# A linear-attention and SwiGLU block: the first two x tiles as column halves ahead of the K weights, and the sum of phi(k) over tiles on GpSimd and VectorE

## The chip, the cores and the metric

The kernel runs on one core of a Trainium2 chip. The metric is the device time of one launch in microseconds (us). Three runs of the kernel before gave 224.91, 223.82 and 224.68 us, a median of 224.68 us. Besides these there is one profiled execution, from which all the views of the profile come.

A core has five engines that run side by side and meet at semaphores: TensorE (PE in the profile; its weight loads are listed apart as PEld), VectorE (DVE), ScalarE (ACT), GpSimd (POOL) and SyncE (SP), which here only issues DMAs. ScalarE issues a few DMAs too. An entry such as SPq or ACTq is the issuing of a DMA by that engine.

## The reference

The input x has 2048 tokens (S) of 512 features (D), in bf16. After a layernorm without scale, two blocks read the same normalised xn, and their outputs are added to x:

```python
def phi(t): return where(t > 0, t + 1, exp(t)) + 1e-6

xn = layernorm(x)                               # eps 1e-5
q, k, v = split(xn @ wqkv)                      # 32 heads of 16
pq, pk = phi(q), phi(k)
kv  = einsum("bhsd,bhse->bhde", pk, v)
z   = einsum("bhsd->bhd", pk)                   # the sum over all tokens
num = einsum("bhqd,bhde->bhqe", pq, kv)
den = einsum("bhqd,bhd->bhq", pq, z) + 1e-6
attn = (num / den) @ wo
ffn  = (silu(xn @ w_gate) * (xn @ w_up)) @ w_down   # F = 1792
out  = x + attn + ffn
```

The change touches z, the sum of phi(k) over the tokens, and the way in which the first x tiles reach the core.

## The kernel before, in words

Tokens lie in 16 tiles of 128 (NT = 16) on the partitions of the on-chip memory. The program is a list of operations. `K.add(engine, fns, r, w)` puts an operation at the end of one engine's instruction stream and derives the semaphore waits from the keys that it reads and writes. So the order in which the Python calls stand is the order on each engine; nothing is reordered later, and an instruction whose wait is not over holds up all that stands behind it on its engine.

**Loads.** The lines from 188 on issue the loads of x and of the weights of K and Q. Tile 0 comes as two column halves, one on SP's queue and one on ACT's. Then SP issues the K weights (`wload("sp", 1)`, 512 KB), tile 3, the Q weights (`wload("sp", 0)`, 512 KB), and tiles 6 to 15. ACT issues tiles 1, 2, 4 and 5, 128 KB each.

**First stage, tiles 0 to 3.** For each tile VectorE computes the statistics (`bn1`, `bn2`, lines 230 and 233), ScalarE the reciprocal standard deviation (`rs`, lines 237 and 239), VectorE the normalised tile (`lna_dve`, line 243). TensorE transposes it in four pieces (`transp`, line 261), and ScalarE evicts the result into xnT (`evac`, line 268). The K projection of the tile follows (`kproj`, line 299: four matmuls). VectorE's order in this stage is: statistics 0, statistics 1, normalisation 0, aggregation 1, statistics 2, normalisation 1, statistics 3, normalisation 2, normalisation 3. TensorE's is: transposes 0, transposes 1, K projection 0, transposes 2, K projection 1, transposes 3, K projections 2 and 3. Ahead of all this TensorE runs NWARM = 9 matmuls on zeros (line 222).

**Middle stage, steps s = 4 to 17.** From tile 4 on GpSimd normalises (`lna_pool`, lines 248 and 251), and a DMA transposes (`dmat`, line 276). A step s has the K projection of tile s, a Q projection (`qproj`, line 310), and the accumulation of xn^T times phi(k) of tile s - 2 in banks 0 to 3 (`gacc`, line 317). phi takes three engines: ScalarE the exponential (line 289), GpSimd the minimum with 1 (line 290), VectorE the combination with the projection in PSUM (line 293). Projections write banks 4 to 7 in turn, so a bank is written again two steps later. Tile 15 is the last that GpSimd normalises, at step 11; from step 12 on it has two minima a step.

**Last stage.** 56 pairs j of gate and up matmuls run (`gu(j)`, line 421: eight matmuls), 14 to each chunk of 512 tokens. ScalarE takes silu of the gate part (line 425), and VectorE multiplies with the up part (`hop(j)`, line 430). The rest of the attention is placed between the pairs:

- after pair 1, `z_sum` (line 454): 16 matmuls with a matrix of ones sum phi(k). Each of the four column groups of TensorE's array takes every fourth tile, and 32 output rows hold the same sum, so bank 1 holds four partial sums, 32 rows each. ScalarE copies it as bf16 (`zhi`), VectorE forms the remainder (`zlo`, line 459). Then `kv_mm` (line 444) with VectorE's mask (line 448);
- after pair 2, `z_mm` (line 466): eight 128x128 matmuls against a matrix of 1/32 (four groups, times zhi and zlo), whose results VectorE spreads into the block columns `Zc` (line 471); then `m_mm` (line 493), of which two follow pair 3;
- after pair 4, `den_mm` (line 476: 16 matmuls), ScalarE's copy (line 480), and four reciprocals on VectorE (`recip`, line 485), each followed by GpSimd's split into rhi and rlo (lines 486 and 487);
- after pairs 7, 10, 13 and 16, `bc_mm` (line 500): the reciprocals are broadcast, and `pqn` (line 508) multiplies them into phi(q), in this pair and the two behind it.

From the second chunk on, `otile` (lines 513 and 517) computes one output tile of the chunk before after the pairs 5, 8, 10 and 13 of a chunk (`O_SLOT`); VectorE adds x (line 523), and SP writes the tile out. The last four tiles follow at the end.

Of the kernel before, what the change touches and what calls it, by code (L numbers as in the profile page):

```python
# [20 lines left out]
HPG = P // DH  # L21
NH = D // DH

NWARM = 9
O_SLOT = {5: 0, 8: 1, 10: 2, 13: 3}


class _Program:
# [76 lines left out]
def bass_parallel_sum__linear_attn_block__swiglu_ffn__prompt_kernel(nc, A_x, A_wqkv, A_wo, B_x, B_w_gate, B_w_up, B_w_down, out):  # L105
    xin = A_x[0]
    oview = out[0]
    K = _Program()
    bf, f32 = dt.bfloat16, dt.float32

    with contextlib.ExitStack() as es:
        E = es.enter_context

        def sb(name, shape, dtype):
            return E(nc.sbuf_tensor(name, shape, dtype))
# [9 lines left out]
        pk = sb("pk", [P, NT, D], bf)  # L125
        pqT = sb("pqT", [P, NG, S], bf)
        hT = sb("hT", [P, 2, NFC, 512], bf)
        zhi = sb("zhi", [P, D], bf)
        zlo = sb("zlo", [P, D], bf)
        ef = sb("ef", [P, 4, D], bf)  # L130
        GT = sb("GT", [P, NDC, D], bf)
        kvT = sb("kvT", [P, NG, P], bf)
# [7 lines left out]
        sil = sb("sil", [P, 2, 512], bf)  # L140
        out_sb = sb("out_sb", [P, 2, D], bf)
        ident = sb("ident", [P, P], bf)
        ones = sb("ones", [P, 32], bf)
        ones32 = sb("ones32", [P, P], bf)
        maskt = sb("maskt", [P, P], bf)
        mask8 = sb("mask8", [P, HPG], bf)
        warm = sb("warm", [P, 512], bf)
# [37 lines left out]


        K.add("act", lambda e: e.preload_act_table_set("natural_log_exp_and_others"))
        for h, eng in ((0, "sp"), (1, "act")):
            load(eng, ("x", 0, h), x_sb[:, 0, h * 256:h * 256 + 256], xin[0:P, h * 256:h * 256 + 256])
        xload("act", 1)  # L190
        wload("sp", 1)
        xload("act", 2)
        xload("sp", 3)
        xload("act", 4)
        wload("sp", 0)
        xload("act", 5)
# [20 lines left out]
        blockmask(("mask8",), mask8[:, :], mask8[:, :], [])  # L217
        K.add("pool", lambda e: e.memset(eps6[:, :], 1e-6), w=[("eps6",)])
        K.add("pool", lambda e: e.memset(ones[:, :], 1.0), w=[("ones",)])
        K.add("pool", lambda e: e.memset(ones32[:, :], 1.0 / 32), w=[("ones32",)])  # L220
        K.add("pool", lambda e: e.memset(Zc[:, :, :], 0.0), w=[("Zc",)])
        K.add("pe", [(lambda e: e.matmul(banks[0][:, :], warm[:, 0:P], warm[:, :], start=True, stop=True))
                     for _ in range(NWARM)], r=[("warm",)], w=[B(0)])


        def xk(t):
            return [("x", t)] if t else [("x", 0, 0), ("x", 0, 1)]

        def bn1(t):
            K.add("dve", lambda e: e.bn_stats(stats[:, t, :], x_sb[:, t, :]), r=xk(t), w=[("st", t)])  # L230
# [91 lines left out]
        def eb_copy(q):  # L322
            sl = slice(32 * q, 32 * q + 32)
            dst = Eb[sl, :].rearrange("p (h e) -> p h e", e=DH)
            src = ident[sl, sl][:, :, None].broadcast_to([32, NH, DH])
            K.add("act", lambda e: e.activation(dst, src, ACT.Copy), r=[("ident",)], w=[("Eb", q)])

        def norm(t):
            bn1(t)
            bn2(t)  # L330
            rs(t)
            lna_pool(t)
            dmat(t)
# [54 lines left out]
        for s in range(4, NT + 2):  # L388
            prev, ends = ends, []
            if s < NT:  # L390
                ends.append(kproj(s))
            for e_ in prev:
                e_()
            for i in SQ[s]:
                ends.append(qproj(i))
            gacc(s - 2)
            if s + 4 < NT:
                norm(s + 4)
            if s in AL:
                AL[s]()  # L400
            if s > 12:
                for e_ in ends:
                    e_()
                ends = []
            if 12 <= s <= 15:
                eb_copy(s - 12)

        for h in (1,):
            fload("sp", "wg", wg, B_w_gate, h)
# [18 lines left out]
        def hop(j):  # L428
            C, fc = j // NFC, j % NFC
            K.add("dve", lambda e: e.tensor_tensor(  # L430
                out=hT[:, C % 2, fc, :], in0=banks[gb(j) + 1][:, :], in1=sil[:, j % 2, :], op=ALU.mult),
                r=[B(gb(j) + 1), ("sil", j % 2)], w=[("hT", C % 2, fc)])


        def gt_evac(c, eng):
            if eng == "act":
                K.add("act", lambda e: e.activation(GT[:, c, :], banks[c][:, :], ACT.Copy), r=[B(c)], w=[("GT", c)])
            else:
                K.add("dve", lambda e: e.tensor_copy(GT[:, c, :], banks[c][:, :]), r=[B(c)], w=[("GT", c)])
# [10 lines left out]
                in1=maskt[:, :][:, None, :].broadcast_to([P, NG, P]), op=ALU.mult),  # L450
                r=[B(0), ("maskt",)], w=[("kvT",)])

        def z_sum():
            K.add("pe", [(lambda e, q=q, t=t: e.matmul(
                banks[1][32 * q:32 * q + 32, :], ones[:, 0:32], pk[:, 4 * t + q, :],
                start=(t == 0), stop=(t == NT // 4 - 1))) for t in range(NT // 4) for q in range(4)],
                r=[("pk", t) for t in range(NT)] + [("ones",)], w=[B(1)])
            K.add("act", lambda e: e.activation(zhi[:, :], banks[1][:, :], ACT.Copy), r=[B(1)], w=[("zhi",)])
            K.add("dve", lambda e: e.tensor_tensor(out=zlo[:, :], in0=banks[1][:, :], in1=zhi[:, :], op=ALU.subtract),
                  r=[B(1), ("zhi",)], w=[("zlo",)])  # L460

        def z_mm():
            fns = []
            for g in range(NG):
                for i, z in enumerate((zhi, zlo)):
                    fns.append(lambda e, g=g, z=z, i=i: e.matmul(
                        banks[1][:, g * P:(g + 1) * P], z[:, g * P:(g + 1) * P], ones32[:, :],
                        start=(i == 0), stop=(i == 1)))
            K.add("pe", fns, r=[("zhi",), ("zlo",), ("ones32",)], w=[B(1)])
# [12 lines left out]

        def recip(q):
            sl = slice(q * P, (q + 1) * P)
            K.add("dve", lambda e: e.reciprocal(rd[:, sl], den[:, sl]), r=[("den",)], w=[("rd", q)])  # L485
            K.add("pool", lambda e: e.tensor_copy(rhi[:, sl], rd[:, sl]), r=[("rd", q)], w=[("rhi", q)])
            K.add("pool", lambda e: e.tensor_tensor(out=rlo[:, sl], in0=rd[:, sl], in1=rhi[:, sl], op=ALU.subtract),
                  r=[("rd", q), ("rhi", q)], w=[("rlo", q)])
# [40 lines left out]
        def otile(t):  # L529
            b = t % 4  # L530
            ogroup(b, t, 0, D)
            oout(b, t, 0, D)

        gt_evac(1, "act")
        gt_evac(0, "dve")
        gt_evac(2, "act")
        gt_evac(3, "dve")
        for j in range(NGU):
            C, fc = j // NFC, j % NFC
            gu(j)  # L540
            if j == 0:
                hop(j)
            elif j == 1:
                z_sum()
                kv_mm()
                hop(j)
            elif j == 2:
                z_mm()
                hop(j)
                m_mm(0)  # L550
                m_mm(1)
            elif j == 3:
                m_mm(2)
                m_mm(3)
                hop(j)
            elif j == 4:
                den_mm()
                hop(j)
                recip(0)
                recip(1)  # L560
            elif j == 5:
                hop(j)
                recip(2)
                recip(3)
            elif j in (7, 10, 13, 16):
                g = (j - 7) // 3
                bc_mm(g)
                hop(j)
                pqn(g, 0)
            else:  # L570
                hop(j)
                if j in (8, 11, 14, 17):
                    pqn((j - 8) // 3, 1)
                    pqn((j - 8) // 3, 2)
                if j in (9, 12, 15, 18):
                    pqn((j - 9) // 3, 3)
# [65 lines left out]
```

## Time and profile before

| what | us |
|---|---|
| median of three runs | 224.68 |
| lowest and highest run | 223.82, 224.91 |
| the profiled execution, its own time | 223.8 |
| its span in the trace | 222.1 |
| GpSimd busy | 35.6 |
| VectorE busy | 101.1 |
| ScalarE busy | 70.0 |

The span is shorter than the device time of the same execution by 1.7 us. The mean granted clock of TensorE over the span is 0.992. The page's row of DMA traffic shows 166 and 356 GB/s in the first two of 40 slices of 5.55 us, and 57 to 63 GB/s in the next three. The issues of the first loads read as follows (issue, time to landing): the halves of tile 0, 2.1 us on SP and 2.2 us on ACT; tile 1, 4.1 us; the K weights, 4.7 us; tile 3, 4.7 us; the Q weights, 6.8 us.

How to read what follows. A row of the timeline has the start, the length, the engine, the line of the kernel, the operation, the output and the inputs with their shapes, the count, and in brackets how long the engine idled before and what ended it. A row of the chain of waits has the start, the length and the engine with its line. A row of the windows gives for each engine the busy time and the number of instructions in that stretch, then TensorE's granted clock as a share of full speed, the busy share of the DMA engines and what they moved. Engines that idle off the chain cost nothing.

### The profile page before, as it was taken

To read this page: it belongs to the slowest core of one execution; us is meant where nothing else is said; L and a number is where in the kernel's file an instruction comes from. 1 tells how busy PE (TensorE), PEld (TensorE's weight loads), DVE (VectorE), ACT (ScalarE), POOL (GpSimd) and SP (SyncE) were. 2 spreads that over 40 slices of the span, in tenths; PEclk is the share of its full clock that TensorE was granted. 3 is DMA by queue.
4 is the path that set the end of the run, shared out by engine and by line. 5 is a ranking of instruction groups with operands and counts; after the bars stand their busy time and mean duration, and the time that the engine had idled before them with its cause. 6 is when DMAs were issued, how large, how long until landed. Compare 5 with 4: busy or idle time off the path is not lost.

```text
span 222.1 us, 2733 instructions
## 1 busy us (share of the span) xinstructions
PE 213.2 (96%) x1043; PEld 97.2 (44%) x1063; DVE 101.1 (46%) x170; ACT 70.0 (32%) x138; POOL 35.6 (16%) x81
## 2 busy tenths in 40 slices
PE   6699999999999999999999999999999999999995
PEld 2344334444543444444444444444444444444454
DVE  2876888555549777733223232422424232232121
ACT  3593566666463322213103131311313220130000
POOL 4069697643005000000000000000000000000000
PEclk9699999999999999999999999999999999999999
DMA  5922399997000000000000000000000000000101
GB/s 166 356 63 57 63 230 258 241 383 226 0 0 3 0 0 0 3 0 24 24 0 27 24 0 0 24 23 3 25 24 0 3 24 0 25 24 3 47 24 47
DMA packets 17485, 13.55 MB, mean 61 GB/s; under 512 B 7232, under 2 KB 17472, under 8 KB 17472
## 3 DMA queue, kind: packets, MB, share of 16 engines
q1 hardware_dynamic: 16752, 12.78, 20.0%
q10 hardware_dynamic: 720, 0.59, 0.8%
q8 instruction: 8, 0.13, 0.3%
q14 instruction: 5, 0.04, 0.1%
HBM read 9.70 MB, written 2.10 MB: 53 GB/s over the span
## 4 chain that ended last, share of the span: by engine, by line
PE 83%; POOL 5%; DMA 4%; DVE 3%; issue 2%; ACT 1%; POOLq 0%; ACTq 0%
PE pb L421 41%; PE pb L517 22%; PE pb L513 6%; PE pb L299 4%; PE pb L310 3%; PE pb L317 3%; DMA xnT<-xn 2%; DMA x_sb<-in_A_x_dram 2%; POOL xn L251 2%; POOL ef L290 2%; PE pb L500 1%; DVE rd L485 1%; DVE stats L230 1%; PE pb L261 1%; PE pb L476 0%
## 5 line engine op out<-in xcount | busy, mean ns | idle before, releaser
L425 ACT ACTIVATE sil<-pb 128x512 bf16<-128x512 f32 x56 | 33.3, 597 | 103.8 <-PE pb L421 102.6
L430 DVE TENSOR_TENSOR hT<-pb,sil 128x512 bf16<-128x512 f32 x56 | 38.6, 688 | 47.2 <-PE pb L421 46.4
L421 PE MATMUL pb<-xnT,wg 128*128 128x512 bf16 x221 | 57.0, 379 | 0.3 <-issue 0.2
L421 PE MATMUL pb<-xnT,wu 128*128 128x512 bf16 x216 | 55.9, 379 | 0.4
L517 PE MATMUL pb<-wd,hT 128*128 128x512 bf16 (+1 forms) x233 | 50.7, 366 | 0.3
L517 PEld LDWEIGHTS pb<-wd,hT 128*128 128x128 bf16 x238 | 23.3, 98 | 25.1
L523 DVE TENSOR_TENSOR out_sb<-pb,x_sb 128x512 bf16<-128x512 f32 (+1 forms) x17 | 11.2, 660 | 49.9 <-PE pb L517 49.9
L421 PEld LDWEIGHTS pb<-xnT,wu 128*128 128x128 bf16 x224 | 21.9, 98 | 26.4
L421 PEld LDWEIGHTS pb<-xnT,wg 128*128 128x128 bf16 x224 | 21.5, 98 | 27.1 <-issue 2.1
L290 POOL TENSOR_SCALAR ef<-ef 128x512 bf16<-128x512 bf16 x32 | 19.5, 615 | 17.0 <-ACT ef L289 16.8
L289 ACT ACTIVATE ef<-pb 128x512 bf16<-128x512 f32 x32 | 18.6, 591 | 8.6 <-PE pb L310 4.6
L299 PE MATMUL pb<-wqkv,xnT 128*128 128x512 bf16 x63 | 17.2, 400 | 0.8 <-DMA xnT<-xn 0.7
L513 PE MATMUL pb<-M,pqT 128*128 128x512 bf16 (+1 forms) x68 | 16.6, 366 | 0.0
L317 PE MATMUL pb<-pk,xn 128*128 128x512 bf16 x62 | 16.2, 379 | 0.3 <-DVE pk L293 0.2
L310 PE MATMUL pb<-xnT,wqkv 128*128 128x512 bf16 x63 | 16.2, 379 | 0.1
L293 DVE SCALAR_TENSOR_TENSOR pk<-pb,ef 128x512 bf16<-128x512 f32 x16 | 10.9, 689 | 7.9 <-POOL ef L290 7.6
L293 DVE SCALAR_TENSOR_TENSOR pqT<-pb,ef 128x512 bf16<-128x512 f32 x16 | 10.9, 689 | 5.2 <-POOL ef L290 5.1
L230 DVE BATCH_NORM_STATS2 stats<-x_sb 128x6 f32<-128x512 bf16 x16 | 10.9, 684 | 3.5 <-DMA x_sb<-in_A_x_dram 3.5
L508 DVE TENSOR_TENSOR pqT<-pb,pqT 128x512 bf16<-128x512 f32 x16 | 10.6, 681 | 0.2 <-PE pb L500 0.2
L299 PEld LDWEIGHTS pb<-wqkv,xnT 128*128 128x128 bf16 x64 | 6.3, 103 | 8.6 <-DVE mv L233 0.9
L513 PEld LDWEIGHTS pb<-M,pqT 128*128 128x128 bf16 x68 | 6.6, 98 | 7.4
L317 PEld LDWEIGHTS pb<-pk,xn 128*128 128x128 bf16 x64 | 6.2, 98 | 8.0 <-DVE pk L293 0.7
(60 smaller groups left out, 75.3 us busy)
## 6 DMA issues: line engine op xcount, KB each, us to landing
out_dram<-out_sb SPq DMA_DIRECT2D x15, 128.0 KB, 1.7
wg<-in_B_w_gate_dram SPq DMA_DIRECT2D x2, 896.0 KB, 6.0
wu<-in_B_w_up_dram SPq DMA_DIRECT2D x2, 896.0 KB, 7.2
wd<-in_B_w_down_dram SPq DMA_DIRECT2D x2, 896.0 KB, 11.4
wqkv<-in_A_wqkv_dram SPq DMA_DIRECT2D x3, 512.0 KB, 4.7
x_sb<-in_A_x_dram SPq DMA_DIRECT2D x11, 128.0 KB, 5.7
x_sb<-in_A_x_dram ACTq DMA_DIRECT2D x4, 128.0 KB, 5.4
wo<-in_A_wo_dram SPq DMA_DIRECT2D x1, 512.0 KB, 4.5
```

Of the source, the lines that this page charges most:

```text
L230: K.add("dve", lambda e: e.bn_stats(stats[:, t, :], x_sb[:, t, :]), r=xk(t), w=[("st", t)])
L289: K.add("act", lambda e: e.activation(buf, banks[b][:, :], ACT.Exp), r=[B(b)], w=[bkey])
L290: K.add("pool", lambda e: e.tensor_scalar(out=buf, in0=buf, scalar1=1.0 + 1e-6, scalar2=0.0, op0=ALU.min, op1=ALU.max), r=[bkey], w=[bkey])
L293: return lambda: K.add("dve", lambda e: e.scalar_tensor_tensor(out=dst, in0=banks[b][:, :], scalar=1e-6, in1=buf, op0=ALU.max, op1=ALU.add ...
L299: K.add("pe", [(lambda e, c=c: e.matmul(banks[b][:, :], xnT[:, c, t * P:(t + 1) * P], wqkv[:, c, D:2 * D], start=(c == 0), stop=(c == NDC ...
L310: K.add("pe", [(lambda e, c=c: e.matmul(banks[b][:, :], wqkv[:, c, g * P:(g + 1) * P], xnT[:, c, C * 512:(C + 1) * 512], start=(c == 0), s ...
L317: K.add("pe", [(lambda e, c=c: e.matmul(banks[c][:, :], xn[:, t, c * P:(c + 1) * P], pk[:, t, :], start=(t == 0), stop=(t == NT - 1))) for ...
L421: K.add("pe", [(lambda e, c=c, b=b, w_=w_: e.matmul(banks[b][:, :], w_[:, c, fc * P:(fc + 1) * P], xnT[:, c, C * 512:(C + 1) * 512], start ...
L425: K.add("act", lambda e: e.activation(sil[:, j % 2, :], banks[gb(j)][:, :], ACT.Silu), r=[B(gb(j))], w=[("sil", j % 2)])
L430: K.add("dve", lambda e: e.tensor_tensor(out=hT[:, C % 2, fc, :], in0=banks[gb(j) + 1][:, :], in1=sil[:, j % 2, :], op=ALU.mult), r=[B(gb( ...
L513: fns = [(lambda e, g=g: e.matmul(banks[bank][:, 0:hi - lo], pqT[:, g, t * P:(t + 1) * P], M[:, g, lo:hi], start=(g == 0), stop=False)) fo ...
L517: fns = [(lambda e, fc=fc: e.matmul(banks[bank][:, 0:hi - lo], hT[:, C % 2, fc, jj * P:(jj + 1) * P], wd[:, fc, lo:hi], start=False, stop= ...
```

## The change

Two parts are changed.

The loads: tiles 0 and 1 both come as two column halves, one half on each of the two queues, and all four stand ahead of the K weights. Tile 3 moves from SP's queue to ACT's, behind tile 2. NWARM goes from 9 to 10.

```diff
-NWARM = 9
-O_SLOT = {5: 0, 8: 1, 10: 2, 13: 3}
+NWARM = 10
+O_SLOT = {7: 0, 9: 1, 11: 2, 13: 3}
...
-        for h, eng in ((0, "sp"), (1, "act")):
-            load(eng, ("x", 0, h), x_sb[:, 0, h * 256:h * 256 + 256], xin[0:P, h * 256:h * 256 + 256])
-        xload("act", 1)
+        for t in (0, 1):
+            for h, eng in ((0, "sp"), (1, "act")):
+                load(eng, ("x", t, h), x_sb[:, t, h * 256:h * 256 + 256], xin[t * P:(t + 1) * P, h * 256:h * 256 + 256])
         wload("sp", 1)
         xload("act", 2)
-        xload("sp", 3)
+        xload("act", 3)
```

The sum of phi(k): GpSimd adds tiles 0 to 9 in fp32 (nine adds, one in each of the steps 12 to 17 and three behind the last step), VectorE tiles 10 to 15 (five adds, behind the hops of pairs 1 to 3) and then both halves into a bf16 tile `zb`, behind the hop of pair 4. What is left for TensorE is the sum over the 128 partitions: four 128x128 matmuls against ones, behind pair 5. zhi, zlo and the 16 matmuls of `z_sum` go.

```diff
+        NZP = 10
+        def z_add(half, i):
+            acc, key = zacc[:, half, :], ("zacc", half)
+            t = NZP * half + i
+            first, fkey = (pk[:, t - 1, :], ("pk", t - 1)) if i == 1 else (acc, key)
+            K.add("dve" if half else "pool",
+                  lambda e: e.tensor_tensor(out=acc, in0=first, in1=pk[:, t, :], op=ALU.add),
+                  r=[fkey, ("pk", t)], w=[key])
...
+            if s >= 12:
+                z_add(0, s - 11)
...
-        def z_sum():
-            K.add("pe", [(lambda e, q=q, t=t: e.matmul(
-                banks[1][32 * q:32 * q + 32, :], ones[:, 0:32], pk[:, 4 * t + q, :],
-                start=(t == 0), stop=(t == NT // 4 - 1))) for t in range(NT // 4) for q in range(4)],
...
+        def z_bf():
+            K.add("dve", lambda e: e.tensor_tensor(out=zb[:, :], in0=zacc[:, 0, :], in1=zacc[:, 1, :], op=ALU.add),
+                  r=[("zacc", 0), ("zacc", 1)], w=[("zb",)])
...
         def z_mm():
-            for g in range(NG):
-                for i, z in enumerate((zhi, zlo)):
-                    fns.append(lambda e, g=g, z=z, i=i: e.matmul(
-                        banks[1][:, g * P:(g + 1) * P], z[:, g * P:(g + 1) * P], ones32[:, :],
-                        start=(i == 0), stop=(i == 1)))
+            K.add("pe", [(lambda e, g=g: e.matmul(
+                banks[1][:, g * P:(g + 1) * P], zb[:, g * P:(g + 1) * P], ones[:, :], start=True, stop=True))
+                for g in range(NG)], r=[("zb",), ("ones",)], w=[B(1)])
...
+        for i in range(7, NZP):
+            z_add(0, i)
```

What stands behind each pair moves accordingly: `kv_mm` stays behind pair 1, `m_mm` behind pairs 2 and 3, `z_mm` goes from pair 2 to pair 5, `den_mm` from pair 4 to pair 6, the reciprocals from pairs 4 and 5 (two each) to pairs 6 (one), 7 (two) and 8 (one), the four `bc_mm` from pairs 7, 10, 13 and 16 to pairs 10, 13, 16 and 19, and the output tiles of a chunk from pairs 5, 8, 10 and 13 to pairs 7, 9, 11 and 13.

```diff
             elif j == 1:
-                z_sum()
                 kv_mm()
                 hop(j)
+                z_add(1, 1)
             elif j == 2:
-                z_mm()
-                hop(j)
                 m_mm(0)
                 m_mm(1)
+                hop(j)
+                z_add(1, 2)
+                z_add(1, 3)
...
             elif j == 4:
+                hop(j)
+                z_bf()
+            elif j == 5:
+                z_mm()
+                hop(j)
+            elif j == 6:
                 den_mm()
                 hop(j)
                 recip(0)
+            elif j == 7:
+                hop(j)
                 recip(1)
-            elif j == 5:
-                hop(j)
                 recip(2)
+            elif j == 8:
+                hop(j)
                 recip(3)
-            elif j in (7, 10, 13, 16):
-                g = (j - 7) // 3
+            elif j in (10, 13, 16, 19):
+                g = (j - 10) // 3
                 bc_mm(g)
```

More of the change, by code (lines that the diff above doesn't have):

```diff
@@ L127, in bass_parallel_sum__linear_attn_block__swiglu_ffn__prompt_kernel @@
         hT = sb("hT", [P, 2, NFC, 512], bf)
-        zhi = sb("zhi", [P, D], bf)
-        zlo = sb("zlo", [P, D], bf)
+        zacc = sb("zacc", [P, 2, D], f32)
+        zb = sb("zb", [P, D], bf)
         ef = sb("ef", [P, 4, D], bf)
@@ L142, in bass_parallel_sum__linear_attn_block__swiglu_ffn__prompt_kernel @@
         ident = sb("ident", [P, P], bf)
-        ones = sb("ones", [P, 32], bf)
-        ones32 = sb("ones32", [P, P], bf)
+        ones = sb("ones", [P, P], bf)
         maskt = sb("maskt", [P, P], bf)
@@ L219, in bass_parallel_sum__linear_attn_block__swiglu_ffn__prompt_kernel @@
         K.add("pool", lambda e: e.memset(ones[:, :], 1.0), w=[("ones",)])
-        K.add("pool", lambda e: e.memset(ones32[:, :], 1.0 / 32), w=[("ones32",)])
         K.add("pool", lambda e: e.memset(Zc[:, :, :], 0.0), w=[("Zc",)])
@@ L226, in xk @@
         def xk(t):
-            return [("x", t)] if t else [("x", 0, 0), ("x", 0, 1)]
+            return [("x", t)] if t > 1 else [("x", t, 0), ("x", t, 1)]
         def bn1(t):
@@ L451, in kv_mm @@
                 r=[B(0), ("maskt",)], w=[("kvT",)])
-        def z_sum():
-            K.add("pe", [(lambda e, q=q, t=t: e.matmul(
-                banks[1][32 * q:32 * q + 32, :], ones[:, 0:32], pk[:, 4 * t + q, :],
-                start=(t == 0), stop=(t == NT // 4 - 1))) for t in range(NT // 4) for q in range(4)],
[L457 to L460, printed above, removed]
-        def z_mm():
-            fns = []
-            for g in range(NG):
-                for i, z in enumerate((zhi, zlo)):
-                    fns.append(lambda e, g=g, z=z, i=i: e.matmul(
-                        banks[1][:, g * P:(g + 1) * P], z[:, g * P:(g + 1) * P], ones32[:, :],
-                        start=(i == 0), stop=(i == 1)))
-            K.add("pe", fns, r=[("zhi",), ("zlo",), ("ones32",)], w=[B(1)])
+        def z_bf():
+            K.add("dve", lambda e: e.tensor_tensor(out=zb[:, :], in0=zacc[:, 0, :], in1=zacc[:, 1, :], op=ALU.add),
+                  r=[("zacc", 0), ("zacc", 1)], w=[("zb",)])
+        def z_mm():
+            K.add("pe", [(lambda e, g=g: e.matmul(
+                banks[1][:, g * P:(g + 1) * P], zb[:, g * P:(g + 1) * P], ones[:, :], start=True, stop=True))
+                for g in range(NG)], r=[("zb",), ("ones",)], w=[B(1)])
             for g in range(NG):
@@ L555, in bass_parallel_sum__linear_attn_block__swiglu_ffn__prompt_kernel @@
                 hop(j)
+                z_add(1, 4)
+                z_add(1, 5)
             elif j == 4:
+                hop(j)
[4 more added lines that the diff above has]
+            elif j == 6:
                 den_mm()
@@ L559, in bass_parallel_sum__linear_attn_block__swiglu_ffn__prompt_kernel @@
                 recip(0)
+            elif j == 7:
+                hop(j)
                 recip(1)
-            elif j == 5:
+                recip(2)
+            elif j == 8:
                 hop(j)
-                recip(2)
                 recip(3)
-            elif j in (7, 10, 13, 16):
-                g = (j - 7) // 3
+            elif j in (10, 13, 16, 19):
+                g = (j - 10) // 3
                 bc_mm(g)
@@ L571, in bass_parallel_sum__linear_attn_block__swiglu_ffn__prompt_kernel @@
                 hop(j)
[L572 to L576, printed above, removed]
+                if j in (11, 14, 17, 20):
+                    pqn((j - 11) // 3, 1)
+                    pqn((j - 11) // 3, 2)
+                if j in (12, 15, 18, 21):
+                    pqn((j - 12) // 3, 3)
             if C >= 1 and fc in O_SLOT:
```

## The prediction

> **What bounds the kernel now.** I read the page first, then the chain of waits in order of time, then the timeline of the first 16 us and of 53 to 72 us, and last the windows of the first 12 us for the clock. The page's first row says that TensorE is nearly always busy:
>
> ```profile
> PE 213.2 (96%) x1043; PEld 97.2 (44%) x1063; DVE 101.1 (46%) x170; ACT 70.0 (32%) x138; POOL 35.6 (16%) x81
> ```
>
> The chain says where that is the bound: from 33.32 us on it is matmul behind matmul, so a matmul removed there is its own time saved. Ahead of it the chain is a pipeline fill (chain of waits; start, length, what):
>
> ```profile
> 1.74 4.96 DMA x_sb<-in_A_x_dram
> 6.73 0.70 DVE stats L230
> ...
> 7.99 0.61 PE pb L261 x4
> 8.60 1.71 PE pb L299 x4
> 10.31 0.43 PE pb L261 x4
> 10.73 1.08 PE pb L299 x4
> 11.81 0.24 PE pb L261 x4
> 12.07 0.60 ACT xnT L268
> ```
>
> The end waits for x tile 2 (issued 1.74, landed 6.70), then for TensorE. See the lengths: four K matmuls take 1.71 us here and 0.86 us in every later row of the chain. From 12 to 33 us GpSimd, VectorE and DMA transposes follow each other with nothing dated from outside, so a shift at 12 us is carried to the end. The windows say why the K matmuls are slow (stretch, length, busy PE, PEld, DVE, ACT, POOL, granted clock, DMA share, GB/s):
>
> ```profile
> 5.00:6.00 1.00, 0.00 (x0) 0.00 (x0) 0.65 (x2) 0.00 (x0) 0.00 (x0) 1.00 1.08 372
> 6.00:7.00 1.00, 0.40 (x4) 0.23 (x4) 0.73 (x4) 0.48 (x3) 0.00 (x0) 1.00 1.08 382
> 7.00:8.00 1.00, 0.01 (x1) 0.01 (x1) 0.97 (x4) 0.80 (x4) 0.00 (x0) 0.81 1.11 353
> 8.00:9.00 1.00, 1.00 (x6) 0.70 (x7) 0.96 (x3) 0.56 (x2) 0.00 (x0) 0.50 1.11 347
> ...
> 11.00:12.00 1.00, 1.00 (x9) 0.62 (x8) 0.68 (x2) 0.86 (x2) 0.06 (x1) 0.98 0.88 281
> ```
>
> TensorE idles after its warm-up matmuls (4.82 us), the clock falls to half at about 7.6 us and comes back at about 11.05, just where the K projections begin.
>
> **Part one, the x tiles.** VectorE is in order: statistics of tile 1 stand ahead of the normalisation of tile 0.
>
> ```profile
> 5.36 0.69 DVE L230 BATCH_NORM_STATS2 stats<-x_sb 128x6 f32<-128x512 bf16 x1 [1.35 <-DMA x_sb<-in_A_x_dram]
> 5.96 0.40 DVE L243 TENSOR_SCALAR xn<-x_sb,mv,rstd 128x512 bf16<-128x512 bf16 x1
> ```
>
> Tile 0's rstd was ready at 4.56, but its normalisation waited for tile 1. Landing: tile 0's halves took 2.1 and 2.2 us from issue; tile 1, whole on ACT's queue beside the 512 KB of K weights, took 4.1. As halves second on each queue (issued about 1.26) it has no K bytes ahead of it. Bounds: 1.26 + 2.1 = 3.4, and 5.35 (no gain); nearest row is the half at 2.1 us, and the stretch 3.0 to 4.0 moved 172 KB while 128 KB are needed, so I take 3.8. Then statistics 1 run at 4.02 (right behind tile 0's, which end at 4.00), normalisation 0 at 4.75, and its transposes come at about 5.25 in place of 6.42.
>
> Tile 2 stays third on ACT, with 64 + 64 + 128 = 256 KB up to its end in place of 320. Tiles 1 and 2 landed 1.35 us apart: ACT's queue gets 95 GB/s beside SP's, so 64 KB are 0.67 us: 6.0 at the latest, 3.8 + 1.35 = 5.2 at the earliest. I take 5.5, near the early end since 1.35 us is a measured spacing. Normalisation 1 ends by 6.85 and tile 1's transposes start at 6.9 (before 7.99).
>
> What pays: K weights go out one issue later (0.41 us) behind 64 KB more, so 5.96 becomes about 6.3; the first K matmul needs the eviction of tile 0's transposes (6.3) and stands behind tile 1's transposes: hidden. Tile 3 moves from SP (landed 6.42) to ACT, 1.35 us behind tile 2: 6.9. Its statistics come free at 6.85, so it is what is late next, by 0 to 0.5 us, part of it beside the K matmuls. Tiles 4 and 5 are behind 64 KB more on ACT; they landed about 8 and 9.3 and were wanted at 10.0 and 10.8: they may get 0.7 us later, nothing on the path. ACT issues six loads in place of five (0.46 us each, free at 3.75), and its first logarithm is due at 4.04: hidden. SP loses tile 3's issue and gains tile 1's half, so the Q weights (2.26) are not later. The tenth warm-up matmul ends by about 5.2, where the transposes come: hidden.
>
> The clock decides the rest. **The rule** (the Trainium skill, "TensorE: Matmul & The Clock Gate", Part 1): a free-running window of about 3.4 us; half rate comes after at least one idle window. The trace agrees on the length (half clock for 7.6 to 11.05 us) but not on idleness: the 3.4 us ahead of 7.6 held 0.6 us of warm-up and 0.4 us of transposes, under 30% busy and not idle, and the clock fell. After the change the same stretch holds about 0.8 us of warm-up, 0.3 + 0.3 us of transposes and 0.6 us of K matmuls, some 55%. By the rule the clock stays up; by the row it may fall still. Sum by the rule: transposes 1 at 6.9 to 7.2, K projection 0 to 8.05, transposes 2 (tile 3 decides) 8.5 to 8.75, K projection 1 to 9.6, transposes 3 to 9.85, ScalarE's evictions to about 10.6: 2.0 us ahead of the eviction that began at 12.07 and ended at 12.67. Sum at half clock: 6.9 + 0.4 + 1.71 + 0.43 + 1.71 + 0.3 = 11.4, a gain of 0.7. I take the rule's side for the forecast, since the one row that speaks against it is half as busy, and keep 0.7.
>
> **Part two, the sum of phi(k).** Removed from the bound stretch:
>
> ```profile
> 56.79 0.98 PE pb L454 x16
> ...
> 60.49 0.45 PE pb L466 x8
> ```
>
> 16 matmuls are 0.98 us; 4 of 8 final ones stay, 0.22. Saved: 1.20 us. ScalarE's zhi and VectorE's zlo go as well, hidden. The denominators move two steps later and the first broadcast three, which bears on one stall:
>
> ```profile
> 71.91 0.40 PE L500 MATMUL pb<-rhi,Eb 32*128 32x512 bf16 x4 [0.38 <-POOL rlo L487]
> ```
>
> Now the fourth reciprocal stands behind the hop of pair 8, 1.8 us after that pair's matmuls, and GpSimd adds 0.9: 2.7, against two pairs of 1.73 = 3.46. The 0.38 goes. Output tiles move within their chunk (slots 7, 9, 11, 13 for 5, 8, 10, 13): the same matmuls, the last slot kept, 3.45 us between tiles against 1.7 us for an output to land. Nothing.
>
> Added on **GpSimd**: nine adds of 128x512 to fp32. No such row. Two-input 128x128 fp32 takes 0.43 us (L487), a one-input cast 0.29, a one-input 128x512 0.615: slope 0.85 ns an element, fixed 0.18, so a two-input element 1.95 ns and the add 1.18 us. Bounds 0.615 and 4 x 0.43 = 1.72. Steps there take 2.59 us, with two minima of 0.61 and this gap:
>
> ```profile
> 48.01 0.61 POOL L290 TENSOR_SCALAR ef<-ef 128x512 bf16<-128x512 bf16 x1 [1.11 <-ACT ef L289]
> ```
>
> 1.18 into 1.11: the next minimum is 0.1 late. Behind it wait VectorE's phi and the bank that TensorE writes two steps on: phi ended 46.76, the bank is written from 48.86, 2 us of cover. At 1.72 GpSimd lags 0.35 us a step, 1.7 after five, still inside. The last four adds end at about 59. **The rule** that speaks against it ("GPSIMD Engine Reference", Engine selection and Performance versus the Vector engine): two-input elementwise work belongs on VectorE, 2.6 cycles an element here; at 1.2 GHz an estimate of 1.11 us plus dispatch. It agrees with the row on the price, but price alone costs nothing while GpSimd idles.
>
> Added on **VectorE**: five adds and one sum. Nearest rows 0.66 and 0.688 us (two-input, PSUM), lower bound 0.39; I take 0.66. Counted from the first gate matmul (53.34): kv mask 4.7 to 5.4, hop 1 to 6.1, add to 6.75, hop 2 to 7.45, two adds to 8.75, hop 3 to 9.45, two adds to 10.75, hop 4 to 11.45, the sum to 12.1. The z matmuls stand behind pair 5, which ends at 12.25. Slack 0.15; at 0.69 an add a stall of about 0.1. Charged: 0.1.
>
> **Sum.** 1.20 + 0.38 - 0.1 = 1.5 us and 2.0 at the front, less 0.2 for tile 3: 3.3. Span 222.1 gives 218.8; 1.7 us lie around it (223.8 for this execution), so 220.5. The median of the runs is 224.68, 0.9 above the profiled one: 224.7 - 3.3 = 221.4.
>
> **Rivals.** (a) The clock still falls: front 0.7, 222.5. For it: it fell at under 30%. Chance 0.28. (b) The halves do not land earlier, since 512 B rows are slow (137 GB/s at a DMA share of 0.76 in a quarter microsecond at 2.5) or tile 3 takes the place of tile 2: front 0, 223.2. Against it: 172 KB moved at 3 to 4. Chance 0.12. (c) GpSimd becomes the bound: lag after five adds is 5 x (a - 1.3), the cover 2 us; it gives back 3.3 when a passes 2.4 us, twice my estimate; at 2.8, 5 x 1.5 - 2 = 5.5 lost and 226.9. For it: nine adds on the slow engine, and a VectorE next door sharing memory; against it: L487. Chance 0.05 for slower than before. Forecast 0.55.
>
> **Numbers.** About 0.5% (1.1 us, 223.6) is what a measurement here can tell from no change. The forecast's own range is 220.3 to 222.2; with (a), most of (b) and an early tile 2 it is 219.9 to 223.4. Faster by more: 0.55 + 0.28 and a little of (b), 0.85; same 0.10; slower 0.05.
>
> **What would show it.** Right: tile 1's statistics start near 4.0; the granted clock stays 1.00 through 8 to 11 us; the last transposed eviction near 10; no TensorE wait before the z matmuls and the first broadcast; GpSimd adds near 1.2 us. Wrong: clock 0.50 in any of those stretches, statistics of tile 3 waiting for DMA beyond 7.4, GpSimd adds over 2 us, or TensorE waiting for phi from 41 to 55 us.

## The result, and the profile after

The changed kernel takes 221.48 us (median of four runs, 221.20 to 221.61) against 224.80 us for the kernel before on the same chip (four runs, 223.82 to 225.76). The ratio is 0.9851, with a 95% interval of 0.9807 to 0.9895. The forecast was 221.4 us. Its profiled execution took 221.42 us with a span of 219.7 us. The kernel before had 223.8 and 222.1, so the spans differ by 2.4 us and the medians by 3.3.

The page's first row of the changed kernel:

```profile
PE 212.6 (97%) x1044; PEld 96.3 (44%) x1044; DVE 104.3 (47%) x175; ACT 69.7 (32%) x137; POOL 45.5 (21%) x89
```

GpSimd is busy 9.9 us more (nine adds of 1.15 us are 10.4), VectorE 3.2 us more, and TensorE is still the bound. The chain of waits of the changed kernel (start, length, what):

```profile
2.22 5.62 DMA x_sb<-in_A_x_dram
7.86 0.71 DVE stats L228
...
10.65 0.60 ACT xnT L266
...
26.69 5.85 DMA xnT<-xn
32.67 1.02 PE pb L297 x4
```

The eviction of the last transposed tile, at 12.07 before, begins at 10.65: 1.42 us won. But the K projection behind the long DMA transpose begins at 32.67, where the kernel before shows this:

```profile
28.16 5.03 DMA xnT<-xn
33.19 0.14 issue
33.32 0.81 PE pb L299 x3
```

Of 1.42 us only 0.65 arrive. The transpose was issued 1.47 us earlier, and it took 0.82 us longer. From there TensorE runs through, and the z part brings the rest. The windows of the changed kernel (columns as in the prediction) have the full clock where the K projections are, and the timeline has tile 0's four K matmuls at 1.03 us from first start to last end, where the kernel before has 1.91:

```profile
7.00:8.00 1.00, 0.30 (x5) 0.30 (x6) 0.75 (x4) 0.50 (x2) 0.00 (x0) 1.00 1.11 374
8.00:9.00 1.00, 0.96 (x6) 0.23 (x3) 0.97 (x3) 0.79 (x2) 0.00 (x0) 1.00 1.10 348
```

```profile
7.94 1.03 PE L297 MATMUL pb<-wqkv,xnT 128*128 128x512 bf16 x4
```

**Three stretches.** Two marks cut every trace in this study: the start of the last transposed eviction (xnT from PSUM on ScalarE, tile 3), and the start of the first gate matmul in the timeline. They give a start, a middle and a tail (span less the second mark). All values are from profiled executions.

| kernel | start | middle | tail |
|---|---|---|---|
| before | 12.07 | 41.10 | 168.93 |
| changed | 10.65 | 41.88 | 167.17 |
| loads part alone | 10.65 | 42.11 | 168.94 |
| z part alone | 12.64 | 41.15 | 167.11 |
| before, 16 warm-ups | 10.80 | 41.22 | 168.88 |
| before, later schedule only | 13.32 | 41.04 | 168.44 |
| before, weights late | 13.38 | 40.51 | 168.91 |
| changed, weights late | 11.88 | 40.57 | 167.15 |
| z part, 16 warm-ups | 11.18 | 41.05 | 167.17 |
| z part, 16 warm-ups, weights late | 11.00 | 40.43 | 167.17 |
| changed, 14 warm-ups | 10.54 | 41.95 | 167.11 |
| changed, 14 warm-ups, weights late | 10.52 | 40.69 | 167.19 |
| the same, tile 2 in halves | 9.87 | 40.63 | 167.20 |

The tail depends on the z part (with its later schedule) alone, to 0.1 us. The start depends on the clock and on x, and the middle on the weight loads and, in an unexpected way, on the x loads.

### The profile page after: what moved, and what is told of

Read it like the earlier page. It is cut to its first block, busy times and chain, and to the rows that moved or that the text cites. A ratio compares the mean times of both kernels' runs of the same rounds, so it can differ in the third digit from the quotient of the medians.

```text
span 219.7 us, 2729 instructions
## 1 busy us (share of the span) xinstructions
PE 212.6 (97%) x1044; PEld 96.3 (44%) x1044; DVE 104.3 (47%) x175; ACT 69.7 (32%) x137; POOL 45.5 (21%) x89
## 4 chain that ended last, share of the span: by engine, by line
PE 84%; DMA 5%; POOL 4%; DVE 2%; ACT 2%; issue 1%; ACTq 0%; POOLq 0%
PE pb L432 44%; PE pb L519 22%; PE pb L515 6%; PE pb L308 4%; PE pb L315 3%; DMA xnT<-xn 3%; DMA x_sb<-in_A_x_dram 3%; PE pb L297 2%; POOL xn L249 2%; POOL ef L288 2%; PE pb L502 1%; DVE stats L228 1%; ACT xnT L266 1%; ACT ef L287 0%; PE pb L478 0%
## 5 line engine op out<-in xcount | busy, mean ns | idle before, releaser
L432 PE MATMUL pb<-xnT,wu 128*128 128x512 bf16 x224 | 57.5, 379 | 0.0
L297 PE MATMUL pb<-wqkv,xnT 128*128 128x512 bf16 x64 | 16.3, 379 | 1.5 <-DMA xnT<-xn 1.5
```

Of the source, the lines that this page charges most:

```text
L297: K.add("pe", [(lambda e, c=c: e.matmul(banks[b][:, :], xnT[:, c, t * P:(t + 1) * P], wqkv[:, c, D:2 * D], start=(c == 0), stop=(c == NDC ...
L432: K.add("pe", [(lambda e, c=c, b=b, w_=w_: e.matmul(banks[b][:, :], w_[:, c, fc * P:(fc + 1) * P], xnT[:, c, C * 512:(C + 1) * 512], start ...
```

## The experiments

The times are medians. The runs came in three groups, each on one chip with its own runs of the kernel before (medians 224.45, 224.46 and 224.97 us). Between groups the ratio to the kernel before says more than the time.

**The loads part alone.**

```diff
-NWARM = 9
+NWARM = 10
+ (the loads of x and K as in the change; z part and order as before)
```

> Only the loads part and the tenth warm-up matmul; the z part as before. Theory A (both parts pay, as in the profile of the change): the last transposed eviction begins about 10.7 instead of 12.07 us, the first K projection behind the long DMA wait about 0.65 us earlier (32.7 for 33.3), and the time falls by 0.7 (0.65 on arrival) to 1.8 (my forecast for this part): 223.0 to 224.1 against 224.8. Theory B (the loads part pays nothing in the end, the DMA transposes take all of it back): within 0.3 us of before. The granted clock stays 1.00 from 7 to 11 us in both.

Measured: 224.19 us (12 runs, 223.12 to 224.61), before 224.45 (31 runs, 223.71 to 225.87); ratio 0.9977 (0.9955 to 0.9999). The 0.26 us are what Theory B expected, and its transposes do take part of the gain back, but neither theory had the clock low in some runs. The profiled execution shows the start of the changed kernel, 10.65, with a transpose of 6.03 us behind it. It took 223.4 us and is one of the faster ones. Seven of the twelve runs have a mean granted clock of 0.992 and took 223.97 to 224.61; the five at 0.999 or more took 223.12 to 224.16. So ten warm-ups do not hold the clock in every run, and that the four runs of the changed kernel all had it at 1.00 was in part luck.

**The z part alone.**

```diff
-NWARM = 10
+NWARM = 9
+ (the loads of x and K as before; z part and order as in the change)
```

> Only the z part: adds on GpSimd and VectorE, four matmuls, the later schedule; loads and nine warm-up matmuls as before. Theory A: 1.5 (forecast) to 1.75 us (what the profile of the change shows behind 52.7 us) faster, 223.1 to 223.3 against 224.8; the granted clock still falls to 0.50 around 8 to 11 us. Theory B (the z part is worth the whole gain of 3.3 us): about 221.5.

Measured: 222.84 us (222.47 to 223.46), ratio 0.9930 (0.9903 to 0.9956). That is 1.6 us, between the two numbers of Theory A. The tail is 1.82 us shorter than before.

**Sixteen warm-ups on the kernel before.**

```diff
-NWARM = 9
+NWARM = 16
```

> The kernel before with sixteen warm-up matmuls in place of nine, nothing else: TensorE is busy up to about 6.2 us, where the first transposes come at 6.4. Theory A (of the loads part, the clock is worth more than the earlier arrival): the clock stays 1.00, the K projection of tile 0 takes 0.86 in place of 1.71 us, the last transposed eviction begins at about 10.6 to 11 and the time falls by 0.5 to 1.3 us. Theory B (earlier arrival is what pays): the eviction begins about 11.8 and the time stays within 0.3 us of before, since statistics and normalisation of tiles 2 and 3 are what is waited for.

Measured: 222.83 us (222.37 to 223.87), ratio 0.9926 (0.9904 to 0.9948): 1.6 us from seven matmuls on zeros, more than Theory A had. Its chain of waits:

```profile
8.55 0.86 PE pb L299 x4
...
10.80 0.60 ACT xnT L268
...
26.84 5.19 DMA xnT<-xn
```

The K projection takes 0.86 us in place of 1.71, and the last eviction begins at 10.80. With no load moved this start is only 0.15 us behind that of the changed kernel, and its transpose takes 5.19 us where the changed kernel's takes 5.85. So most of what the loads part brings is the clock, and more warm-up brings that with no load moved.

**Only the later schedule.**

```diff
-O_SLOT = {5: 0, 8: 1, 10: 2, 13: 3}
+O_SLOT = {7: 0, 9: 1, 11: 2, 13: 3}
...
-            elif j == 4:
+            elif j == 6:
                 den_mm()
+ (reciprocals and broadcasts at the later pairs too; sum and final matmuls of z as before)
```

> The kernel before, with its 16 sum matmuls and eight final ones, but with the denominators, reciprocals, broadcasts and output tiles at the later pairs of the change. Theory A: only the wait of 0.38 us ahead of the first broadcast goes: 0.3 to 0.5 us faster, 224.3 to 224.5. Theory B (the later schedule is where most of the z part comes from): 1 us or more. If the schedule costs something by itself: slower than before.

Measured: 224.55 us (223.45 to 225.33), ratio 0.9998 (0.9974 to 1.0022): nothing that the median can tell. In the table the tail is 168.44, 0.49 shorter than before, as Theory A has it; the start of that execution, 13.32, hides it. Its window and its chain, which do not fit each other:

```profile
9.00:10.00 1.00, 1.00 (x4) 0.30 (x2) 0.46 (x2) 0.92 (x3) 0.00 (x0) 1.00 1.12 352
```

```profile
9.01 1.71 PE pb L299 x4
...
11.15 1.71 PE pb L299 x4
```

The view says 1.00, while four matmuls take 1.71 us, twice the 0.86 of full speed. The trace of this execution holds no entry of the clock at all before or behind, and the view then prints 1.00. Nor did a clock that was up fall: the nine warm-up matmuls are slow from the first to the last (minimum/median/maximum in ns), where the shortest of the kernel before takes 379:

```profile
L222 PE MATMUL pb<-warm x9: 610/634/634, 1.3 to 4.6; 128*128 128x512 bf16 x9
```

A clock of 1.00 in this record is therefore no proof; the length of the matmuls is. The single runs agree: the seven with a mean clock of 1.00 took 224.51 to 225.33 us, the five with 0.992 only 223.45 to 224.14.

**The changed kernel with the weight loads behind the last transpose.**

```diff
-        AL = {5: lambda: fload("sp", "wg", wg, B_w_gate, 0), 7: lambda: fload("sp", "wu", wu, B_w_up, 0),
-              9: lambda: wload("sp", 2), 10: lambda: woload("sp")}
+        AL = {11: late}     # wg and wu first halves, V weights, wo, in this order
```

> The changed kernel, with the loads of the first halves of the gate and up weights, of the V weights and of wo issued behind the last DMA transpose (step 11) and not between the transposes (steps 5, 7, 9, 10). Theory A (the transposes take 5 to 6 us in place of 2.5 because they share the DMA engines with 896 KB loads, and this takes back half of what the loads part gains): the long transposes go to about 2.5 to 3 us, the waits of 0.36 and 1.18 us ahead of the K projections go, and the time falls by 1.0 to 1.6 us to 219.9 to 220.5. Theory B (GpSimd's chain of normalisation and minima sets the pace there, the transposes only end last): the same waits come back with another releaser, and the time stays within 0.4 us of 221.5. Against both: the later weights are late for the first gate matmuls or for the V product, slower than 221.5.

Measured: 221.00 us (220.31 to 221.33), ratio 0.9852 (0.9820 to 0.9884), no other than that of the changed kernel (0.9851); only two of its six runs, 220.31 and 220.40, reach Theory A's range. The middle is 40.57 in place of 41.88, 1.3 us shorter, as Theory A says; but in the profiled execution the clock fell, and the start is 11.88. The trace's record of the clock has the rise at 4.47 us and the fall at 7.88; the windows between these marks:

```profile
4.47:7.88 3.41, 1.62 (x13) 0.74 (x12) 1.76 (x6) 2.08 (x8) 0.00 (x0) 1.00 1.09 369
7.88:11.30 3.42, 3.10 (x12) 1.12 (x11) 2.69 (x7) 2.08 (x5) 0.00 (x0) 0.50 1.11 348
```

In the 3.4 us ahead of the fall TensorE was busy for 1.62 us, 47%.

**The kernel before with the same later weight loads.**

> The kernel before with the same later weight loads. Theory A: the wait of 0.44 us ahead of the K projection at 33.3 us and most of that at 24.9 go: 0.4 to 1.0 us faster than before (224.5), less than for the changed kernel, since before the transposes held it up less. Theory B: within 0.3 us of before.

Measured: 224.44 us (223.38 to 224.82), before 224.46; ratio 0.9997 (0.9974 to 1.0021). The middle of its one profiled execution is 0.6 us shorter than before, but the median does not move. Its start in that execution is a late one (13.38), with K projections of 1.71 us. Nine of its twelve runs have a recorded clock of 1.00 and took 224.09 to 224.82 us, so they may be of the kind that the later schedule's profile shows; whether its runs drew late clocks more often than those of the kernel before, these runs do not tell.

**GpSimd's adds twice.** Each of the nine adds is followed by one of the same size into a tile that nobody reads, so the output does not change.

```diff
+            if not half:
+                K.add("pool", lambda e: e.tensor_tensor(out=zdup[:, :], in0=acc, in1=pk[:, t, :], op=ALU.add),
+                      r=[key, ("pk", t)], w=[("zdup",)])
```

> The changed kernel with each of GpSimd's nine adds followed by a second add of the same size into a tile that nobody reads: the added cost doubled, 2.31 us a step. By my rival (c), with lag = 5 x (2.31 - 1.3) = 5 us after five adds against 2 us of cover: about 3 us slower than the changed kernel, 224.5, with TensorE waiting for phi between 43 and 55 us. If the cover is larger than I worked out, or the adds hide wherever they stand: less than 1 us slower.

Measured: 229.14 us (227.53 to 230.39), ratio 1.0231 (1.0184 to 1.0277): 7.7 us above the changed kernel's median, not 3. Its profiled execution is the fastest of the six, 227.53 us, with a span 6.1 us longer than that of the changed kernel. GpSimd's timeline (start, length, engine, line, operation):

```profile
46.85 1.19 POOL L289 TENSOR_SCALAR ef<-ef 128x512 bf16<-128x512 bf16 x2
48.01 1.15 POOL L335 TENSOR_TENSOR zacc<-zacc,pk 128x512 f32<-128x512 f32 x1
49.23 1.15 POOL L338 TENSOR_TENSOR zdup<-zacc,pk 128x512 f32<-128x512 f32 x1
50.35 1.19 POOL L289 TENSOR_SCALAR ef<-ef 128x512 bf16<-128x512 bf16 x2
```

A step takes 3.50 us on GpSimd, and the last minimum begins at 57.37 where the changed kernel has 52.55: 4.8 us late, the lag that I had worked out (5). TensorE waits for phi three times, 0.74 us up to 51.75, 0.74 up to 55.26 and 1.61 up to 58.77: 3.1 us, the 3 that I had expected. VectorE's evictions for the V product stand behind the late phi in its queue, so that product starts at 59.96 in place of 56.15, 3.8 us late. What I had wrong is what comes behind it. The rest of the adds meet VectorE's, and TensorE waits once more:

```profile
62.64 1.61 POOL L335 TENSOR_TENSOR zacc<-zacc,pk 128x512 f32<-128x512 f32 x1
...
66.88 2.60 DVE L335 TENSOR_TENSOR zacc<-zacc,pk 128x512 f32<-128x512 f32 x2
```

```profile
58.77 1.04 PE L437 MATMUL pb<-xnT,wu 128*128 128x512 bf16 x4 [1.61 <-DVE pqT L292]
...
70.74 0.40 PE L474 MATMUL pb<-ones,zb 128*128 128x128 bf16 x4 [1.95 <-DVE zb L470]
```

Side by side, GpSimd's add takes up to 1.61 us in place of 1.15 and VectorE's 1.04 to 1.53 in place of 0.69. The z matmuls start at 70.74 in place of 64.81, 5.9 us late. The slower runs also show a lower mean clock (0.985 at 230.3 us, 1.00 at 227.5); whether it fell in these waits or in the fill, as it can with ten warm-ups, was not looked into.

**The z part with sixteen warm-ups, no load of x moved.**

> The z part alone on the loads of before, with sixteen warm-up matmuls in place of nine. Theory A (what the loads part of the change brings is the clock, and more warm-up brings it without any load moved): 222.84 of the z part alone less the 1.6 us that sixteen warm-ups gave on the kernel before, 221.2, not slower than the change (221.48). Theory B (the earlier arrival of tile 1 matters by itself): 0.5 us or more slower than the change, 222 or above.

Measured: 220.92 us (220.72 to 221.11), ratio 0.9855 (0.9822 to 0.9887): Theory A, not slower than the change. That it is faster is not shown: the median is 0.56 us lower, but the two did not run together, and the ratios to the kernel before (0.9851 for the change) do not differ. In the profiled execution the long transpose takes 5.02 us.

**The same with the weight loads behind the last transpose.**

> The z part, the loads of x as before, sixteen warm-up matmuls, and the weight loads behind the last DMA transpose. Theory A (with the clock kept up, the transposes beside the 896 KB loads are what is left of the fill): 0.6 to 1.1 us faster than the same kernel with the weight loads between the transposes (220.92), 219.8 to 220.3. Theory B (the later weight loads pay only for kernels with the moved x loads): within 0.3 us of 220.9.

Measured: 220.45 us (220.29 to 220.67), ratio 0.9810 (0.9781 to 0.9840). The 0.47 us are a little under what Theory A expected; they compare two chips, and the middles of the two profiled executions differ by 0.62 us.

**The changed kernel with fourteen warm-ups.**

> The changed kernel with fourteen warm-up matmuls in place of ten. The clock should stay up in every run. Theory A (at equal clock the moved loads are worth nothing or cost a little, since tile 3 now lands last at 7.8 us and the long transpose takes 0.8 us more): 220.9 to 221.5, not faster than the z part on the old loads with sixteen (220.92). Theory B (the moved loads are worth 0.5 us or more at equal clock): 220.4 or less.

Measured: 221.50 us (221.28 to 221.89), ratio 0.9858 (0.9828 to 0.9889). At equal clock the moved loads win 0.64 us at the start (10.54 against 11.18) and lose 0.90 in the middle (41.95 against 41.05), and the ratio is that of the z part with sixteen (0.9855): Theory A.

**Both costs of the fill away: fourteen warm-ups, weight loads late.**

> The changed kernel with fourteen warm-up matmuls and the weight loads behind the last DMA transpose: both costs of the fill that the traces show, taken away together. The two fastest runs of the changed kernel with the later weight loads, in which the clock stayed up, were 220.31 and 220.40: Theory A expects 220.1 to 220.5 in all runs, with no run near 221. If the clock has nothing to do with the spread of that kernel (220.3 to 221.3), the spread stays.

Measured: 219.95 us (219.76 to 220.34), ratio 0.9789 (0.9759 to 0.9820). No run is near 221. The weight loads had cost this kernel 1.55 us (221.50 less 219.95, the same chip). With the weights out of the way the moved loads at last pay: 219.95 against 220.45, also on this chip, though of the 0.48 us that they win at the start the profiled executions keep only 0.2 (spans 218.4 and 218.6).

**Tile 2 in halves as well.**

```diff
-        for t in (0, 1):
+        for t in (0, 1, 2):
...
-        xload("act", 2)
```

> As the changed kernel with fourteen warm-ups and the later weight loads, but tile 2 too comes as two column halves ahead of the K weights, so that tile 3 is the next on ACT's queue. Theory A (tile 3's landing at 7.8 us is what bounds the start): tile 3's statistics begin near 6.8 in place of 7.86, the last transposed eviction about 0.8 us earlier, 219.4 to 219.9. Theory B (the K weights, another 64 KB later, or the clock take its place): within 0.3 us of the kernel without it (220.1 to 220.5).

Measured: 219.18 us (218.80 to 219.97), ratio 0.9758 (0.9724 to 0.9792), the fastest of this study. Tile 3's statistics, in its timeline and in that of the changed kernel:

```profile
6.29 0.69 DVE L227 BATCH_NORM_STATS2 stats<-x_sb 128x6 f32<-128x512 bf16 x1
```

```profile
7.86 0.69 DVE L228 BATCH_NORM_STATS2 stats<-x_sb 128x6 f32<-128x512 bf16 x1 [0.21 <-DMA x_sb<-in_A_x_dram]
```

They begin at 6.29 and wait for no DMA, and the last eviction begins at 9.87, 0.65 us earlier than without the halves: Theory A, somewhat exceeded. What is late next is the warm-up itself: its chain opens with fourteen warm-up matmuls up to 6.56 us.

## Why the prediction was right, and where it was not

The time and the sign were right, and one of its two parts was right for the reason given. The other came out right by luck, since two errors offset each other: the loads won less than forecast, and most runs of the kernel before were slower than the profiled one.

- **The z part** (forecast 1.5 us): right. The part alone brought 1.6 in the medians, and the tails 1.76 to 1.82. The tails split it: 0.49 belongs to the later schedule (forecast 0.38), and about 1.3 to the removed matmuls (forecast 1.20). The stall of 0.1 us ahead of the z matmuls did not come:

```profile
61.35 3.45 PE pb L432 x16
64.81 0.22 PE pb L469 x4
```

  Nor does TensorE wait ahead of the first broadcast, as it did for 0.38 us before:

```profile
74.68 0.40 PE L502 MATMUL pb<-rhi,Eb 32*128 32x512 bf16 x4
```

- **The price of the adds**: right. GpSimd's was forecast at 1.18 us, VectorE's at 0.66; the tile view of the changed kernel has (minimum/median/maximum in ns):

```profile
L334 POOL TENSOR_TENSOR zacc<-zacc,pk x8: 1152/1154/1156, 43.6 to 56.8; 128x512 f32<-128x512 f32 x8
L334 DVE TENSOR_TENSOR zacc<-zacc,pk x4: 680/688/693, 59.5 to 62.4; 128x512 f32<-128x512 f32 x4
```

  The nine adds hid. GpSimd's last ends at about 57.98 and VectorE's first begins at 58.28. With 0.3 us between them they did not meet; the prediction charged nothing for a meeting, and the run with the adds twice shows what one can cost.
- **Tile 1 early** (statistics forecast at 4.02, transposes 0 at 5.25): right in the main, 3.93 and 5.50. Two costs that it called hidden lie behind the 0.25 us between: ScalarE issued its six loads until 4.21 and not 3.75, so its first logarithm began at 4.33 in place of 4.04, and in this execution all ten warm-up matmuls ran slow (607 to 634 ns each), so the transposes stood directly behind them. Neither reaches the end, as tile 3 comes later.
- **Tiles 2 and 3** (forecast 5.5 and 6.9): wrong in size. Tile 2's statistics began at 6.44 and tile 3's at 7.86, both waiting for the DMA. The step that failed is "near the early end since 1.35 us is a measured spacing". In the run with fourteen warm-ups and the same loads tile 2's came at 5.65, so this landing moves by 0.8 us from run to run; tile 3 was the bound in both (7.75 there). Statistics of tile 3 waiting for DMA beyond 7.4 was one of the signs that the prediction named for being wrong. The last eviction came at 10.65 where I had 10.0 (10.2 with what I charged for tile 3).
- **The clock**: it stayed up, as forecast, but the ground was weak. I took the rule of the Trainium skill ("TensorE: Matmul & The Clock Gate", Part 1: half rate after at least one idle window) over the one row that spoke against it. The row was right: in the changed kernel with later weights the clock fell behind 3.4 us that were 47% busy, and in the loads part alone it was low in seven of twelve runs. Rival (a) deserved more than 0.28. A limit on the busy share does not follow either: with GpSimd's adds twice (the same ten warm-ups) the clock came up at 5.17, the next 3.41 us were as busy, and the K matmuls behind them still ran at full speed (1.03 us for four at 9.27):

```profile
5.17:8.58 3.41, 1.61 (x14) 0.76 (x12) 2.16 (x7) 2.08 (x6) 0.00 (x0) 1.00 1.10 363
```

- **"With nothing dated from outside, so a shift at 12 us is carried to the end"**: wrong, the step that failed outright. 0.78 us of the 1.42 were lost in the middle, in the long transpose that stands beside an 896 KB weight load. With the weight loads behind the transposes the middle is 1.3 us shorter, and most of what the x loads win does arrive (0.5 us in the medians). Why the transpose takes 5.85 to 6.03 us in all four kernels with the moved x loads, and 5.01 to 5.19 in the five without (all with the weight loads between), is open. It is not the time of its issue: 26.74 us in the loads part alone, 26.84 with sixteen warm-ups on the kernel before.
- **The sum**: I had 3.3 us, and the spans show 2.4. The forecast held since I set the 3.3 against the median of the kernel before, 0.9 us above its profiled execution. That 0.9 is what the changed kernel does not have: its runs lie within 0.2 us of its profiled one. The clock is the likely reason: with full-speed K projections the start lies between 9.87 and 11.18 in the profiled executions, with slow ones between 11.88 and 13.38, by when the slow stretch falls. The kernel before, and all three profiled variants that keep its x loads and its nine warm-ups, have one of the latter, and 12.07 in the profile that I had is the earliest of these four. That each single run of it is spread by this was not profiled. The parts do not add up to the whole either: alone they brought 1.6 and 0.3 us, 1.9 in sum. The five runs of the loads part without the low clock (median 223.49) were 1.0 faster, which makes 2.6; the rest lies within the intervals of the ratios.
- **Rival (b)**: in part true, tile 3 takes the place of tile 2. **Rival (c)**: the lag and the cover were right (3.1 us of waits for phi at twice the cost); what it lacked is that the late adds meet VectorE's and slow both.

## What to carry to other kernels

A sum that is spread over engines with idle time was worth the matmuls that it took off the bound engine, and a wait that the later schedule removed; the two engines that share it should not add at the same time. A gain in the pipeline fill must be followed through every later transfer before it is counted: here more than half of it was gone behind the DMA transposes that share the queue with weight loads. At full clock the moved x loads brought nothing with the weight loads between the transposes (ratios 0.9858 with them, 0.9855 without), and 0.5 us with the weight loads behind. Before loads are moved to keep TensorE's clock up, more warm-up matmuls are the cheaper test: seven gave 1.6 us here.

## What the runs showed of the hardware that was not expected

- In the four profiled executions in which TensorE's clock came up and fell again, the fall came 3.41 us behind the rise: 4.22 and 7.63 us (before), 5.44 and 8.85 (z part alone), 4.20 and 7.61 (before, weights late), 4.47 and 7.88 (changed, weights late). The rise moves between executions, and the fall with it. TensorE was 26 to 47% busy in these 3.41 us; in one execution in which the clock held it was 47% as well. What decides is open.
- The record of the granted clock can be empty, and the views then print 1.00: so in the later schedule only, with four K matmuls in 1.71 us, and in the run with tile 2 in halves, with full-speed ones.
- DMA transposes landed 2.4 us after their issue at the median and 4.1 at most with no weight load between them, and up to 5.9 with weight loads of 512 and 896 KB on the same queue (first the changed kernel, then with the weights late; minimum/median/maximum from 13 to 45 us):

```profile
DMA to landing us min/median/max: 2.4/3.3/5.9
```

```profile
DMA to landing us min/median/max: 2.4/2.4/4.1
```

- VectorE and GpSimd, both adding two tiles in SBUF (the memory on the chip), slowed each other: from 0.69 to between 1.04 and 1.53 us on VectorE, from 1.15 to as much as 1.61 on GpSimd. The Trainium skill ("GPSIMD Engine Reference", Specifications) names this contention for VectorE instructions with two SBUF inputs, without a size.
